# Tiles 8 to 15 of x transposed by VectorE blocks and sixteen SBUF transfers, in a kernel whose task order is written out

## The chip, the cores and the metric

The kernel runs on one core of one Trainium2 chip. The metric is device time in microseconds (us); less is better. Times are medians over runs of one program.

The core has five engines that follow their own instruction queues and wait for each other through semaphores: TensorE (PE in the profile; its weight loads are PEld), VectorE (DVE), ScalarE (ACT), GpSimd (POOL) and SyncE (SP). SBUF is the memory that all work on, in 128 partitions; PSUM holds matmul results in eight banks. Transfers are issued from the queues of SP, ACT and POOL and carried out by 16 DMA engines.

## The reference

```python
S, D, F = 2048, 512, 1792                     # x: [1, S, D] in bf16
g = sigmoid((x * gate_w).sum(-1, keepdims=True))
X = rfft2(x.astype(float32)) * (w_r + 1j * w_i)     # w: [S, D/2+1]
a = irfft2(X, s=(S, D)).astype(bfloat16)
h = x @ w1 + b1                                # w1: [D, F]
b = (h * tanh(softplus(h))) @ w2               # Mish; w2: [F, D]
out = g * a + (1 - g) * b
```

Two branches read the same x: a spectral filter (a two-dimensional real Fourier transform, a product with complex weights W, and the transform back), and a dense layer with Mish between two matrix products. A gate per row mixes them.

## The kernel before, in words

x is held as `xo`, 16 tiles of 128 rows by 512 features. Both branches contract over features first, so they need x with the features in partitions: `xT`, four feature blocks (even and odd features of the lower and the upper half) by 2048 rows. Before, TensorE makes all of `xT`: a matmul with the identity per 128x128 block (L476, tasks `tr0a` to `tr14`, two tiles each), and an eviction from PSUM by DVE (tasks `evx`, L404).

The dense branch goes in four chunks c of 512 rows. `mm1_c_ft` (L773) makes 128 of the 1792 hidden features for a chunk, four matmuls of 128x512 over the four feature blocks; `mish_c_ft` (ACT, L788) evicts them into `act`, which has three buffers, so chunk 3 uses that of chunk 0 again. For chunk 0 the first four are done in parts (`mm1a0_0` and so on, two matmuls of 128x256 each) as x comes in. `mm2_t_part` (L803) makes the output of tile t from 14 hidden blocks, seven with each half of w2; `bev_t` (L755, L756) scales it, `sum_t` adds the spectral part in `ga`, and `store` writes two tiles at a time. Tiles 14 and 15 take `fin` (L815) in one step.

The spectral branch is a chain: `ts`, `td` (DVE, sums and differences of `xT` halves per four tiles), `a1` (L512, transform along features), `eg`, `e1` (evictions), `s1` (L538, first stage along rows), `e2` (eviction), `r1w` (a store to scratch memory), `r1r` (the load back, regrouped, after all sixteen stores), `s2` (L635), `wm` and `wz` (the product with W on DVE and POOL), `s2i` (L695), `e4`, `r2w` and `r2r` (a second trip through scratch), `s1i` (L723), `e5`, `a1i` (L734), `gc`, `sa` (L739, L745) and `sb` (L409, on POOL but for the last tiles), which leave `ga`. The gate comes from `gdot` (DVE, L554), `gpow`, `gadd`, `gcol`, `omg`. `rcw` (L584), `weff`, `wab` prepare edge columns of W.

Nothing decides the order at run time. The program is a list of tasks with their reads and writes (`G.add`); `schedule` reads the string `ORDER`, two digits for each task, with the engine where a task may run on several and the PSUM bank, and appends the task to its engine's queue. Each engine then runs its queue in order, with a wait for each semaphore that a task depends on (L864). A transfer is a task on the queue that issues it (L374); one that waits holds up everything behind it on that queue.

SP's queue begins with x, w1 and the tables, then 18 loads of W (`ld_Wp`, `ld_Wm`, `ld_Wz`), the table `ld_rf`, the two halves of w2 (`ld_w2_0`, `ld_w2_1`), and then the sixteen stores `r1w` and the loads `r1r`.

Of the kernel before, what the change touches and what calls it, by code (L numbers as in the profile page):

```python
# [257 lines left out]
ORDER = (  # L258
    "0M0N0U047050P060O07080Q2z09000S0A010R0B0C0D0T020E0F030V0G0H0W0I0J0X0x60z50Y0yv0Z0K10v1146v212v1H30a1366l51I6q0"
    "14v0L7011Jv6m6n6w1Kv0b716o0c726p731L40d1M36r1N0e1W50f6s6t741Ov1V70g1560h1Pv1X6x0i6y6u16v7510j1Qa1Zv6z0k1701av1"  # L260
    "971Yv77318v761R41Av781B61Sv7920l0m0n7B01fv7A0o7D10p7C1gv0q1D70r1Cv7E1h30s1r42j1s61j7F20t21v0u1Ev7H00v22v1i17G1"
    "T7J31kv7I1U1lv2451F27K7L01mv1t1Gv2371uv7N47M1vv252Ov7O7b127v1wa2D37c2k28a26v7d07f22Nv7e2l1b67g1n42m2E11ca7h22F"
    "7j01d1ov1e7i1x62Hv7k1p342922Gv1ya1q7l52Av2Ia2Q41z2P17m2Z67n0202n2R2b2B2J22Tv7o2a72C2Sv7p12Ka2Uv2cv7r67q2dv2L2V"
    "27s2M2ev7t02Wv2f67u7v12o2X2ga2p7x52Y7w2h2q7z07y2i2r816802s8F1822t3578H48G362u398J28I373A8L58K2v3B8N63C388M0w8P"
    "18O2w8R28Q2x8T02y8S3D4308U3E63Mv8V38X13Nv8W8Y3Rv3Pg313F7P03G323Qv3Og7Q333H3Tg3Z33Sg7Ra3a13b8Z63iv3I57S08a3mv3J"
    "3jv7T3K3L3U3nv3kg3V47Ua7V33c3Xa3Wv3d3pg3Y3e03v43f3og3w644v7W3lg3x3y49v7Y13g7Xv3z3h3q45v7Z48v46g4028307aa4147g3"
    "r4843ta4Bg3sv4Ag3u4H485a4I24Qv86642434J4K4C4Uv4L874Rv89188a4Vv4Sg4D44Wg4M38b24Ea4N4Fa4Tg8c8A4G4Xg8d74O8Ba4P4Y8"
    "C08e4Z28f14av4ba8D8g4c8t18Ev8v28u8x08w4d8z18y4e9124f904g933929549497096992989B79A4h39C4p59D04qv4ia4x64r59E4yv4"
    "j75534s5D45L156a5Ev5T04z65Ma8h24u504t4k5Uv4wg5N14m5F34vg525V55O8i4l9fv5G5Q4ng515b78k04og8jv5W5P54g5I5Sg5H5768l"
    "5ca9ev5853g9g599F75Rg5A8mv5Kg9H49G5Y5Cg5d65X9J09I9hv5e9lv5j45r39K5Jg8n75sv5ka5Bg9kv5g5z35ag9m6745f5l568a5t19iv"  # L270
    "8o60v5m5hg9j5u5o5ig5v6908pa6F45n5Zg6135w8q26Ga5qg629nv6A645pg8r6B9ov635xg9p6C6N46V59qv6Oa9L78sv5yg6Wa66g6P69rv"
    "6X46Q6H26Eg6d09s6Y9M6S6I6Dg6R6ea6K65g6J9O19Nv6Ug6a6Mg6Z9P9uv9tv6cv9v6f56Tg9Qa9R46bv6g9xv6h6Lg9S6i9wv6kv9y9V06j"
    "g9T9U9Y29W9b79X9Z9a9c9d"
)
# [17 lines left out]
def _build(nc, A_x, A_w_r, A_w_i, B_x, B_w1, B_b1, B_w2, gate_w, out):  # L292
# [8 lines left out]
    with es:  # L301
        def sb(name, shape, dt):
            return es.enter_context(nc.sbuf_tensor(name, shape, dt))

        xo = sb("xo", [128, NT, 512], BF)
        xT = sb("xT", [128, 4, NT * 128], BF)
        Tg = sb("Tg", [128, 8192], BF)
# [157 lines left out]

        for t0, h in ((0, 0), (0, 1), (2, 0), (2, 1), (4, None), (6, None), (8, None), (10, None), (12, None), (14, None)):
            pt = _Ps(SPEC[::-1])
            hs = (0, 1) if h is None else (h,)
            c0, nc_ = 2 * hs[0], 2 * len(hs)

            def f_tr(e, t0=t0, c0=c0, nc_=nc_, pt=pt):
                ins = None
                for i in range(2):
                    for c in range(c0, c0 + nc_):
                        o, d0 = ((c - c0) * 2 + i) * 128, 256 * (c // 2) + c % 2
                        ins = e.transpose(psb[:, pt.bank, o:o + 128], xo[:, t0 + i, d0:d0 + 255:2], ident[:, :])  # L476
# [14 lines left out]
        for t in range(NT):  # L491
            if t % 4 == 0:
                G.cur_prio = PR["sp"] + 0.9
                h = t // 4
                cols = slice(512 * h, 512 * h + 512)
                for (nm, o, op) in (("s", 0, ALU.add), ("d", 2, ALU.subtract)):
                    tt(f"t{nm}{h}", lambda o=o, hb=h % 2: Tb[:, hb, o:o + 2, :], lambda cols=cols: xT[:, 0:2, cols],
                       lambda cols=cols: xT[:, 2:4, cols], op, 1024, rate=2.0,
                       reads=[("xT", 4 * h + i, q) for i in range(4) for q in range(2)], writes=[("T", h % 2, nm)])
            if t % 2 == 0:  # L500
# [3 lines left out]
                for half in range(2):  # L504
                    pa = pas[half]

                    def f_a1(e, pa=pa, hb=hb, t=t, half=half):
                        ins = None
                        for i in range(2):
                            j0 = 128 * (t % 4 + i)  # L510
                            for r in range(2):
                                ins = e.matmul(ps[:, pa.bank, 256 * i:256 * i + 256].rearrange("p (s m) -> p s m", s=4)[:, r:4 - r:3 - 2 * r, :],  # L512
                                               Tb[:, hb, 2 * r + half, j0:j0 + 128], FMs[:, 2 * half + r, :], start=True, stop=True)
# [250 lines left out]
        for c in range(NCH):  # L764
            hb = c % 3
            G.cur_prio = PR["mm1"] - c
            for ft in range(NFT):
                pd = _Ps(DENSE[c])

                def f_mm1(e, c=c, ft=ft, pd=pd, cols=(0, 512), ks=range(4)):  # L770
                    ins = None
                    for i in ks:
                        ins = e.matmul(ps[:, pd.bank, cols[0]:cols[1]], w1_sb[:, i, 128 * ft:128 * (ft + 1)], xT[:, i, 512 * c + cols[0]:512 * c + cols[1]],  # L773
                                       start=(i == 0), stop=(i == 3))
                    return ins
# [11 lines left out]
                G.add(f"mish_{c}_{ft}", "act", act_dur(512, True),
                      lambda e, ft=ft, pd=pd, hb=hb: e.activation(act[:, hb, ft, :], ps[:, pd.bank, :], AF.Mish, bias=b1f[:, ft:ft + 1]),  # L788
                      reads=[("pm", c, ft), "b1f"], writes=[("act", hb, ft)], frees=[pd], prio=PR["mish"])
# [148 lines left out]
```

## Time and profile before

| | |
|---|---|
| median of 3 runs | 130.08 us (129.92 to 130.22) |
| profiled execution, first to last instruction | 128.0 us, TensorE's granted clock 1.000 |
| TensorE busy | 124.4 us, 97% |
| DVE, ACT, POOL busy | 92.2, 68.9, 54.4 us |
| moved by DMA | 20.11 MB |

For the profiled execution the profile gives the span alone; what lies around the span is outside the profile. In rows of a group, the columns are the line of the code, engine, operation, output and inputs with their shapes, the count, then busy time in us and the mean of one in ns, then the engine's idle time just before them and what ended it. In the chain and the timelines the columns are start and length in us. "To landing" is the time from the start of a transfer's issue to the arrival of its data. DVE and ACT instructions overlap at their ends: the step from one start to the next is about 0.08 us shorter than the length of one.

### The profile page before, as it was taken

How to read it: one execution, taken by the hardware profiler on the slowest of the kernel's cores; microseconds unless marked ns; L12 is line 12 of the kernel's file. 1: busy time of each engine (PE TensorE's matmuls, PEld its weight loads, DVE VectorE, ACT ScalarE, POOL GpSimd, SP SyncE). 2: the span in 40 equal slices, each digit the busy share in tenths (PEclk: the TensorE clock that was granted, in tenths of full speed). 3: DMA queues.
4: the chain of work that ended last, by engine and by line, in shares of the span. 5: the costliest groups of instructions: out<-in, count | busy, mean ns of one | idle time of the engine just before them, and what ended most of it. 6: DMA issues, size and time to landing. Idle time of an engine off the chain costs nothing.

```text
span 128.0 us, 2725 instructions
## 1 busy us (share of the span) xinstructions
PE 124.4 (97%) x1046; PEld 67.9 (53%) x1046; DVE 92.2 (72%) x176; ACT 68.9 (54%) x113; POOL 54.4 (42%) x82
## 2 busy tenths in 40 slices
PE   7899999999999999999999999999999999999992
PEld 5698566545444444444444444444674457464482
DVE  0359997999989929998957900500399799999872
ACT  1339377889978784224024274487873475462300
POOL 4000000001000996979688394000038986998120
DMA  3999999999976398002304105449600204022231
GB/s 76 346 390 394 303 185 185 173 272 354 334 235 202 99 384 356 0 0 61 108 0 133 38 0 164 133 104 351 239 0 5 82 0 164 3 87 82 82 123 41
DMA packets 18653, 20.11 MB, mean 157 GB/s; under 512 B 1488, under 2 KB 15696, under 8 KB 18512
## 3 DMA queue, kind: packets, MB, share of 16 engines
q1 hardware_dynamic: 17792, 19.15, 49.7%
q10 hardware_dynamic: 816, 0.79, 1.9%
q8 instruction: 8, 0.13, 0.5%
q14 instruction: 5, 0.04, 0.1%
q0 software_dynamic: 32, 0.00, 0.0%
HBM read 13.64 MB, written 6.29 MB: 156 GB/s over the span
## 4 chain that ended last, share of the span: by engine, by line
PE 94%; DMA 3%; SPq 0%; DVE 0%; issue 0%
PE ps L803 38%; PE ps L773 38%; DMA xo<-in_A_x_dram 3%; PE ps L734 3%; PE ps L723 3%; PE ps L512 3%; PE ps L538 3%; PE ps L476 3%; PE ps L695 2%; PE ps L635 2%; SPq L374 0%; DVE xo L815 0%; PE ps L652 0%; PE ps L484 0%; PE ps L425 0%
## 5 line engine op out<-in xcount | busy, mean ns | idle before, releaser
L773 PE MATMUL ps<-xT,w_sb 128*128 128x512 bf16 (+1 forms) x240 | 52.9, 365 | 0.0
L803 PE MATMUL ps<-w_sb,act 128*128 128x512 bf16 (+2 forms) x252 | 51.6, 355 | 0.0
L788 ACT ACTIVATE act<-ps,b1f 128x512 bf16<-128x512 f32 x56 | 38.4, 688 | 18.5 <-PE ps L773 17.3
L803 PEld LDWEIGHTS ps<-w_sb,act 128*128 128x128 bf16 x252 | 22.7, 98 | 22.3 <-issue 0.8
L773 PEld LDWEIGHTS ps<-xT,w_sb 128*128 128x128 bf16 x240 | 22.3, 98 | 21.2 <-issue 0.6
L409 POOL TENSOR_TENSOR Tg<-Qb 128x256 bf16<-128x256 f32 x29 | 22.1, 790 | 21.9 <-DVE Qb L745 21.8
L409 POOL TENSOR_TENSOR Zb<-Qb 128x510 bf16<-128x510 f32 x16 | 19.8, 1268 | 5.1 <-DVE Qb L409 5.0
L409 DVE TENSOR_TENSOR Qb<-ps,WT 128x1024 f32<-128x1024 f32 x16 | 18.8, 1213 | 3.4 <-PE ps L635 3.4
L755 ACT ACTIVATE xo<-ps,omg 128x512 bf16<-128x512 f32 x8 | 5.5, 687 | 18.4 <-PE ps L803 10.1
L745 DVE SCALAR_TENSOR_TENSOR Qb<-ps,gcol,Qb 128x256 f32<-128x256 f32 x32 | 13.7, 475 | 1.5 <-ACT Qb L739 1.0
L404 DVE CAST Ybuf<-ps 128x1024 bf16<-128x1024 f32 x7 | 8.6, 1222 | 7.1 <-PE ps L695 6.7
L409 DVE TENSOR_TENSOR Abuf<-ps,Tg 128x512 bf16<-128x512 f32 x16 | 10.4, 685 | 2.4 <-PE ps L512 2.1
L576 POOL COPY wrv<-WT 128x32 bf16<-128x32 bf16 x2 | 0.4, 223 | 26.1 <-DMA WT<-in_A_w_i_dram 26.1
L405 ACT ACTIVATE Ybuf<-ps 128x1024 bf16<-128x1024 f32 x9 | 9.1, 1021 | 4.3 <-PE ps L695 4.3
L554 DVE SCALAR_TENSOR_TENSOR Tg<-xo,Tg 128x512 bf16<-128x512 bf16 x16 | 11.0, 688 | 0.3
L404 DVE CAST Zb<-ps 128x512 bf16<-128x512 f32 x6 | 4.1, 687 | 8.9 <-PE ps L723 8.9
L404 DVE COPY xT<-ps 128x1024 bf16<-128x1024 bf16 (+1 forms) x10 | 5.6, 579 | 5.4 <-PE ps L476 5.4
L409 DVE TENSOR_TENSOR xo<-xo,Tg 128x512 bf16<-128x512 bf16 x14 | 8.5, 615 | 0.3 <-ACT xo L755 0.3
L739 ACT ACTIVATE Qb<-ps,gcol 128x256 f32<-128x256 f32 x16 | 7.0, 475 | 2.7 <-PE ps L734 1.6
L405 ACT ACTIVATE Zb<-ps 128x512 bf16<-128x512 f32 x10 | 5.7, 596 | 4.6 <-PE ps L723 3.2
L598 POOL TENSOR_TENSOR ch<-wq 128x32 f32<-128x32 f32 x1 | 0.6, 624 | 12.5 <-DVE wq L593 12.5
L476 PE MATMUL ps<-ident,xo 128*128 128x128 bf16 x64 | 5.1, 225 | 0.5 <-DMA xo<-in_A_x_dram 0.5
(59 smaller groups left out, 92.8 us busy)
## 6 DMA issues: line engine op xcount, KB each, us to landing
Abuf<-scr SPq DMA_DIRECT2D x8, 512.0 KB, 5.4
scr<-Ybuf SPq DMA_DIRECT2D x16, 128.0 KB, 3.9
scr<-Ybuf SPq DMA_DIRECT2D x4, 512.0 KB, 3.8
w_sb<-in_B_w_dram SPq DMA_DIRECT2D x2, 896.0 KB, 13.6
out_dram<-xo SPq DMA_DIRECT2D x7, 256.0 KB, 2.0
xo<-in_A_x_dram SPq DMA_DIRECT2D x3, 512.0 KB, 7.7
rt<-c_rt SPq DMA_DIRECT2D x2, 512.0 KB, 8.5
WT<-in_A_w_r_dram SPq DMA_DIRECT2D x7, 128.5 KB, 10.4
```

The source lines that it names most:

```text
L404: fs = {"dve": ("dve", dve_dur(n, rate=rate), lambda e: e.tensor_copy(out=dst(), in_=src())), "act": ("act", act_dur(n), lambda e: e.activ ...
L405: "act": ("act", act_dur(n), lambda e: e.activation(dst(), src(), AF.Copy))}
L409: f = lambda e: e.tensor_tensor(out=o(), in0=i0(), in1=i1(), op=op)
L476: ins = e.transpose(psb[:, pt.bank, o:o + 128], xo[:, t0 + i, d0:d0 + 255:2], ident[:, :])
L512: ins = e.matmul(ps[:, pa.bank, 256 * i:256 * i + 256].rearrange("p (s m) -> p s m", s=4)[:, r:4 - r:3 - 2 * r, :], Tb[:, hb, 2 * r + half ...
L554: lambda e, t=t: e.scalar_tensor_tensor(out=junk, in0=xo[:, t, :], scalar=1.0, in1=gwb, op0=ALU.mult, op1=ALU.mult, accum_out=gdot[:, t:t ...
L739: lambda e, t=t, sl=sl, p5=p5: e.activation(gC[:, sl, :].rearrange("p (i n) -> p i n", i=2), ps[:, p5.bank, :].rearrange("p (i n) -> p i n ...
L745: lambda e, t=t, sl=sl, p5=p5, o=o, op=op: e.scalar_tensor_tensor(out=st1[:, sl, o::2, :], in0=ps[:, p5.bank, :].rearrange("p (i n) -> p i ...
L755: G.add_multi(f"bev_{t}", [("act", act_dur(512, True), lambda e: e.activation(xo[:, t, :], ps[:, pd.bank, :], AF.Copy, scale=omg[:, t:t + ...
L773: ins = e.matmul(ps[:, pd.bank, cols[0]:cols[1]], w1_sb[:, i, 128 * ft:128 * (ft + 1)], xT[:, i, 512 * c + cols[0]:512 * c + cols[1]], sta ...
L788: lambda e, ft=ft, pd=pd, hb=hb: e.activation(act[:, hb, ft, :], ps[:, pd.bank, :], AF.Mish, bias=b1f[:, ft:ft + 1]),
L803: ins = e.matmul(ps[:, pd.bank, cs_], act[:, hb, ft, 128 * tl:128 * (tl + 1)], w2_sb[:, ft, cs_], start=(ft == 0), stop=(ft == NFT - 1))
```

## The change

Tiles 0 to 7 of x are transposed as before, into the first half of `xT`. For tiles 8 to 15, each of eight `tp` tasks is one DVE transpose of a whole tile in blocks of 32x32, written to the third buffer of `act`, where Mish of chunk 2 has not yet written. Block by block this leaves rows and features exchanged inside each 32x32 block, but the blocks in the wrong partitions. Sixteen transfers `sh`, one for each pair of 32-partition groups, 64 KB each, put them in place in the second half of `xT`; each waits for all eight transposes. POOL issues eight and ACT eight. The second half of `xT` has another order of rows (32-row groups of all tiles together), so `ts` and `td` of tiles 8 to 15 become two DVE instructions each, `mm1` of chunks 2 and 3 reads through a pattern, and their Mish puts the rows back in order. Every reader of tiles 8 to 15 waits for all sixteen transfers, and so do the first eight Mish of chunk 2, which overwrite the buffer.

`gdot` gets two scratch outputs in turn, loses its wait for the end of `e1`, and `mm2_15` waits for the other tiles of its chunk.

`ORDER` is new throughout. The engine queues that follow from it differ among other things in this: `mm1a0_1` and `mm1a0_0` stand ahead of the transposes of tiles 2 and 3; all `tp` stand on DVE ahead of the evictions of tiles 4 to 7 (`tp9 tp10 e1p_2 tp11 tp8 tp13 tp12 tp14 tp15 evx6 evx4 e1m_2 td1 ts1 e2_0`); ACT runs `mish_0_8 sh12 sh30 sh32 sh33 mish_0_12 sh13 sh10 mish_1_5 sh31 mish_1_2 sh11 eg_6`; SP runs `ld_gw ld_Wp00 r1w0a`, the other loads of W with `r1w0b` and `ld_ri` among them, then `r1w6b ld_rf r1w6a r1w4a ld_w2_0 ld_w2_1` and the other stores; and TensorE has `mm2_3_0` directly behind `s1_14`, ahead of `s1_10` and `s1_12`.

```diff
 ORDER = (
...
 )
-GD_N = 8
+SHQ = ("pool", "act", "pool", "act")
...
-        xT = sb("xT", [128, 4, NT * 128], BF)
+        xT = sb("xT", [128, 8192], BF)
...
-        junk = Tg[:, 6144:6656]
+        junk = (Tg[:, 6144:6656], Tg[:, 7168:7680])
...
+        xTp = xT[:, 0:4096].rearrange("p (q s) -> p q s", q=4)
+        xTb = xT[:, 4096:8192].rearrange("p (a q t j) -> p q a t j", a=4, q=4, t=8)
+        Zb32 = act[:, 2].rearrange("p f s -> p (f s)")[:, 0:4096]
+        Zw = Zb32.rearrange("p (b h e t j) -> p t h b e j", b=4, h=2, e=2, t=8)
...
-        for t0, h in ((0, 0), (0, 1), (2, 0), (2, 1), (4, None), (6, None), (8, None), (10, None), (12, None), (14, None)):
+        for t0, h in ((0, 0), (0, 1), (2, 0), (2, 1), (4, None), (6, None)):
...
+        for t in range(8, NT):
+            G.add(f"tp{t}", "dve", dve_dur(512), lambda e, t=t: e.transpose(
+                Zw[:, t - 8], xo[:, t, :].rearrange("p (b j e) -> p b e j", b=8, e=2)),
+                reads=[("x", t)], writes=[("Z", t)])
+        shs = []
+        for b in range(4):
+            for a in range(4):
+                shs.append(dma(f"sh{b}{a}", xT[32 * b:32 * b + 32, 4096 + 1024 * a:5120 + 1024 * a], Zb32[32 * a:32 * a + 32, 1024 * b:1024 * b + 1024],
+                               reads=[("Z", t) for t in range(8, NT)], writes=[("xB", b, a)], nbytes=65536, queue=SHQ[b], tail=1.9, bw=250e3))
+        XB = [("xB", b, a) for b in range(4) for a in range(4)]
...
+                    for e_ in range(2):
+                        xs = [xTb[:, e_ + 2 * i, :, 4 * h - 8:4 * h - 4, :] for i in range(2)]
+                        tt(f"t{nm}{h}{e_}", lambda o=o, e_=e_, hb=h % 2: Tb[:, hb, o + e_, :].rearrange("p (t a j) -> p a t j", t=4, a=4),
+                           lambda xs=xs: xs[0], lambda xs=xs: xs[1], op, 512, rate=2.0,
+                           reads=XB, writes=[("T", h % 2, nm, e_)])
...
-            G.cur_prio = PR["gate"] if t >= GD_N else 60.0
+            G.cur_prio = PR["gate"]
...
-                  reads=[("x", t), "gw"], writes=[("gd", t), "junk"], lock=True, deps=e1s[14] if t >= GD_N else ())
+                  reads=[("x", t), "gw"], writes=[("gd", t), ("junk", t % 2)], lock=True)
...
+                        o = ps[:, pd.bank, cols[0]:cols[1]]
+                        ins = e.matmul(o if c < 2 else o.rearrange("p (a t j) -> p a t j", a=4, t=4), w1_sb[:, i, 128 * ft:128 * (ft + 1)],
+                                       xTp[:, i, 512 * c + cols[0]:512 * c + cols[1]] if c < 2 else xTb[:, i, :, 4 * c - 8:4 * c - 4, :],
                                        start=(i == 0), stop=(i == 3))
...
+                      lambda e, c=c, ft=ft, pd=pd, hb=hb: e.activation(
+                          act[:, hb, ft, :].rearrange("p (t a j) -> p t a j", t=4, a=4),
+                          ps[:, pd.bank, :].rearrange("p (t a j) -> p t a j" if c < 2 else "p (a t j) -> p t a j", t=4, a=4),
+                          AF.Mish, bias=b1f[:, ft:ft + 1]),
+                      reads=[("pm", c, ft), "b1f"], writes=[("act", hb, ft)], frees=[pd], prio=PR["mish"],
+                      deps=shs if c == 2 and ft < 8 else ())
...
-                       alloc=pd if part == 0 or t == NT - 1 else None, deps=(mm2s[c][-1:] if t == NT - 1 and part else []))
+                       alloc=pd if part == 0 or t == NT - 1 else None, deps=(mm2s[c][-1:] if t == NT - 1 else []))
```

More of the change, by code (lines that the diff above doesn't have):

```diff
@@ L258 @@
 ORDER = (
[L259 to L273, printed above, removed]
+    "0M0P040050600070Q0108090A0B0C0D0N0E0F0G0H0I0x10J0yv0R0O0K0U020S0z50L7A37511120T031347F612v10a7K70V7614v0W7B1av"
@@ new lines @@
+    "1X01Zv7L0X1Y77787G797H7C1c21l47M1b51n7R01d1ev7D1fv7E7P11gv7V41A7Q7I1m20Y7N7T51B1ov1C1737S7b17h07O7X7197W1E7U1D"
+    "1F0Z1G7J7f418v0a7c1557Z616v7i7Y1N1R1h00b1T1pv1Q1V1W1wv8178538D51vv1iv1S7g1O2842721J7z0341qv1L861U807v1833361j1"
+    "M290c7x038330d7w8B22Bv3A1K7d10e0f820g1H0h7y1I7a1x72Ca1P0i1z1k2Av8H0352Iv8C2Jv1y40w8768j77e8Z220v8p10j8I2Hv883J"
+    "21v2L02Kv8422v2gv2V68E3C0k2D32W50l2fv0m8k2N2M72X8d02hv0n0o2Yv0p2Ea2Zv0q8F62Pv8J38q0r2342iv8a2Ov8G8e24v0s2t12u2"
+    "1r62Qv2G0t2v1sa3O8L02F372xv252ya8t52R62j18f42wv2l0u8M2Sv3E8g8r22k00v2z62av2nv398u7s12b430a2mv1t2oa3B3P68s8n72T"
@@ new lines @@
+    "1u2U8K2p232263G313Q2ca2qv3D7p08h67q2e8943F8v52d3H8o8b72r3I2s8A8c8i7m23T3R3K7t8w3X33S3V3Y63L3M8l58m7n3a7j53Z3hv"
+    "3gv3b3c33U3N3jg7ua3lv7ra3kv7k3ig7la3u03t63d7oa3mg9F43w3ng3v8Q33x8z543v8R9042v46v9G8Sa3y744g3e45g47v4F44G09J24P"
+    "v8x68W33z4H4I4Ov3f3W8y49g3o3p4408X4148g4Sv9K4J4A4Qg3qa3rv4Tv4B49N29L04Ca3s4K14Dv4b44L4Rg4kv4c64Ug4M9O9D28T18Ya"
+    "4Vg4e4d4f4g34N4W9M4lv8U4ng4h4E9V04i9E4pv4mg4ov4rg4X24Za9464j954Ya4qg4s8Vv4a9W4t14vv9108N79T54ua9d1929P29Z39Q4w"
+    "9e9U9H48O9I4x51252a4y5919X55345P29a93v5Av5B08Pv5X15H3977544z565Qa5596a5n25C5Iv5J45Ya5R65f39Y5K5v15E5Z55D5S5ov5"
@@ L496, in _build @@
                 for (nm, o, op) in (("s", 0, ALU.add), ("d", 2, ALU.subtract)):
-                    tt(f"t{nm}{h}", lambda o=o, hb=h % 2: Tb[:, hb, o:o + 2, :], lambda cols=cols: xT[:, 0:2, cols],
-                       lambda cols=cols: xT[:, 2:4, cols], op, 1024, rate=2.0,
-                       reads=[("xT", 4 * h + i, q) for i in range(4) for q in range(2)], writes=[("T", h % 2, nm)])
+                    if h < 2:
+                        tt(f"t{nm}{h}", lambda o=o, h=h: Tb[:, h, o:o + 2, :], lambda cols=cols: xTp[:, 0:2, cols], lambda cols=cols: xTp[:, 2:4, cols], op, 1024, rate=2.0,
+                           reads=[("xT", 4 * h + i, q) for i in range(4) for q in range(2)], writes=[("T", h, nm, e) for e in range(2)])
+                        continue
+                    for e_ in range(2):
[3 more added lines that the diff above has]
+                           reads=XB, writes=[("T", h % 2, nm, e_)])
             if t % 2 == 0:
@@ L514, in f_a1 @@
                         return ins
-                    pe(f"a1{half}_{t}", 4 * mm(128), f_a1, reads=[("T", hb, "s"), ("T", hb, "d"), "FD"], writes=[("pa", t, half)], alloc=pa,
+                    pe(f"a1{half}_{t}", 4 * mm(128), f_a1, reads=[("T", hb, nm, half) for nm in "sd"] + ["FD"], writes=[("pa", t, half)], alloc=pa,
                        deps=e1s.get(t - 4, ()) if half == 0 else (), prio=PR["sp"] + 0.1 - 0.1 * half)
@@ L784, in _build @@
                 else:
-                    pe(f"mm1_{c}_{ft}", 4 * mm(512), f_mm1, reads=[("xT", 4 * c + i, q) for i in range(4) for q in range(2)] + [("w1", ft, 0), ("w1", ft, 1)],
+                    pe(f"mm1_{c}_{ft}", 4 * mm(512), f_mm1, reads=(XB if c >= 2 else [("xT", 4 * c + i, q) for i in range(4) for q in range(2)]) + [("w1", ft, 0), ("w1", ft, 1)],
                        writes=[("pm", c, ft)], alloc=pd, deps=mm2s.get(c - 3, ()), prio=pr_m)
                 G.add(f"mish_{c}_{ft}", "act", act_dur(512, True),
-                      lambda e, ft=ft, pd=pd, hb=hb: e.activation(act[:, hb, ft, :], ps[:, pd.bank, :], AF.Mish, bias=b1f[:, ft:ft + 1]),
-                      reads=[("pm", c, ft), "b1f"], writes=[("act", hb, ft)], frees=[pd], prio=PR["mish"])
+                      lambda e, c=c, ft=ft, pd=pd, hb=hb: e.activation(
[4 more added lines that the diff above has]
+                      deps=shs if c == 2 and ft < 8 else ())
             G.cur_prio = PR["mm2"] - c
```

9 lines of the change are left out of this document (6 added, 3 removed).

## The prediction

> **What bounds the kernel now.** I read the page first (busy shares, chain), then the chain of waits in order of time, then the engines' timelines around each moved step.
>
> ```profile
> span 128.0 us, 2725 instructions
> ...
> PE 124.4 (97%) x1046; PEld 67.9 (53%) x1046; DVE 92.2 (72%) x176; ACT 68.9 (54%) x113; POOL 54.4 (42%) x82
> ...
> PE 94%; DMA 3%; SPq 0%; DVE 0%; issue 0%
> ```
> ```profile
> 5.57 0.40 PE ps L476 x4
> ...
> 7.12 1.75 PE ps L773 x16
> ...
> 12.16 0.89 PE ps L476 x16
> ...
> 20.23 0.22 PE ps L512 x4
> 20.45 0.86 PE ps L773 x4
> ...
> 26.75 0.87 PE ps L538 x4
> ...
> 47.36 0.56 PE ps L635 x32
> ...
> 49.75 3.02 PE ps L803 x14
> ...
> 79.14 0.57 PE ps L695 x32
> ...
> 90.83 0.45 PE ps L723 x8
> ...
> 119.56 6.13 PE ps L803 x56
> ...
> 125.71 0.35 DVE xo L815
> ```
>
> The chain is one engine. From 5.57, when tiles 2 and 3 of x have landed, to 125.69 (119.56 + 6.13) TensorE never waits for anybody; DVE, ACT and POOL feed it just in time. So matmul time that goes away is time gained, but nothing stands idle that could swallow a new wait: a transfer or an eviction that comes later than TensorE reaches its reader is lost time in full.
>
> **What is removed.** The program of after has 32 of the 64 transposes (L476). The chain prices sixteen at 0.89, so 32 cost 1.78 us. Two two-matmul groups of L773 also move ahead of the transposes of tiles 2 and 3, into the wait for x: four matmuls of 128x256 at 1.75/16 are 0.44, of which I count 0.3, since they overrun the landing a little. TensorE: -2.1 us. Four DVE evictions of 1024 columns go too.
>
> **What is added on VectorE.** Eight 32x32-block transposes, 512 columns each, `tp13 tp12 tp14 tp15` being the last four; they stand in front of the evictions `evx6` and `evx4` of tiles 6, 7, 4, 5.
>
> ```profile
> L374 SPq DMA_DIRECT2D xo<-in_A_x_dram x1: 777/777/777, 5.5 to 5.5; - x1
> ...
> DMA to landing us min/median/max: 9.5/9.5/9.5
> ```
> ```profile
> 4.85 0.76 DVE L404 COPY xT<-ps 128x512 bf16<-128x512 bf16 x2 [4.85 <-PE ps L476]
> ...
> 9.83 1.29 DVE L409 TENSOR_TENSOR Abuf<-ps,Tg 128x512 bf16<-128x512 f32 x2 [1.41 <-PE ps L512]
> ...
> 13.02 1.28 DVE L404 COPY xT<-ps 128x1024 bf16<-128x1024 bf16 x2
> 14.39 1.22 DVE L404 CAST Ybuf<-ps 128x1024 bf16<-128x1024 f32 x1
> ```
>
> No row shows this transpose. Below, it costs what a packed 512-column copy does (two in 0.76: 0.34 from start to start); above, what a 1024-column cast does (1.2). I take the 512-column row that moves one element at a time: two in 1.29, so 0.6 from start to start, 0.69 in all. Tiles 12 to 15 land at 5.5 + 9.5 = 15.0 (the loads ahead of them are the same), so the four end at 15.0 + 4 x 0.6 + 0.1 = 17.5, and the two evictions (0.6 each) at 18.8. When does TensorE want them? At `mm1_1_3`. I count its queue from 5.7: 24 transposes (1.33), 28 matmuls of 256 (3.06), nine `mm1` of four (20.45 row: 0.864 each, 7.78), four `a1` groups (0.22 each), `s1_0` (26.75 row: half of 0.87) and one small one: 13.5, so 19.2. (The same count over before's queue meets 49.75 within 0.3.) Hidden, with 0.4 to spare; at 1.2 each the four end at 19.9, the evictions at 21.2, and 2.0 us are lost. [...]
>
> **The sixteen transfers.** Each waits for all eight transposes. Eight are issued by POOL, eight by ACT between its Mish evictions.
>
> ```profile
> L374 POOL DMA_DIRECT2D braw<-in_B_b_dram x1 | 0.8, 785 | 0.8 <-POOLq L923 0.8
> ```
> ```profile
> 0.80 1.94 ACTq L374 DMA_DIRECT2D w_sb<-in_B_w_dram  x3
> ...
> 11.61 1.28 ACT L788 ACTIVATE act<-ps,b1f 128x512 bf16<-128x512 f32 x2
> ```
> ```profile
> out_dram<-xo SPq DMA_DIRECT2D x7, 256.0 KB, 2.0
> ...
> w_sb<-in_B_w_dram ACTq DMA_DIRECT2D x3, 256.0 KB, 4.9
> ```
> ```profile
> L864 PEldq EVENT_SEMAPHORE  x30: 51/51/517, 2.8 to 103.6; - x30
> ```
>
> First reader on TensorE is `mm1_2_5`: eleven `mm1` (9.5) and four `a1` groups (0.9) behind `mm1_1_3`, so 29.6. POOL: 0.785 an issue in the one row there is (a smaller load); I take 0.9, so the eighth issue starts at 17.5 + 6.3 = 23.8. Landing of 64 KB inside SBUF has no row; between the 2.0 of a quiet store and the 4.9 of a load in a full queue I take 3 from the issue's start: 26.8. ACT: eight issues at 0.65 (5.2), seven Mish at 0.6 and 1.2 of smaller evictions reach `eg_4`, whose bank `mm1_2_5` takes, at 28.1. Both hidden; POOL's margin, 2.8, is gone when an issue costs over 1.3, and each 0.1 beyond is 0.7 lost. Sixteen semaphores are read two at a time: eight wait instructions of 0.051 with gaps, 0 to 0.8, taken as 0.3, as only a matmul or two cover them.
>
> **What moves on SP's queue** is the dear part. Before, all eighteen loads of W, then both halves of w2, stand ahead of the first store to scratch. In after, `r1w0a` stands behind the first load of W, and `r1w0a` waits for `e2_0`, which DVE reaches behind the transposes: 17.5, two evictions, three more 0.6 steps and a cast of 1.2: 21.8. Seventeen loads of W queue behind it. And `ld_w2_0` stands behind `r1w4a`, which waits for `e2_4`, the eviction of `s1_4`.
>
> ```profile
> 7.55 5.84 SPq L374 DMA_DIRECT2D WT<-in_A_w_r_dram  x9
> 13.43 6.73 SPq L374 DMA_DIRECT2D WT<-in_A_w_i_dram  x9
> ...
> 20.82 2.59 SPq L374 DMA_DIRECT2D w_sb<-in_B_w_dram  x2
> ```
> ```profile
> 14.50:27.00 12.50, 12.50 (x96) 7.11 (x94) 11.76 (x22) 8.89 (x17) 0.00 (x0) 1.00 1.11 185
> ```
> ```profile
> L374 SPq DMA_DIRECT2D scr<-Ybuf x8: 614/616/617, 35.4 to 40.0; - x8
> ```
> ```profile
> L374 SPq DMA_DIRECT2D Abuf<-scr x1: 344/344/344, 42.3 to 42.3; - x1
> ...
> DMA to landing us min/median/max: 4.0/4.0/4.0
> ```
> ```profile
> L374 SPq DMA_DIRECT2D Abuf<-scr x1: 432/432/432, 43.6 to 43.6; - x1
> ...
> DMA to landing us min/median/max: 6.7/6.7/6.7
> ```
>
> Seventeen issues at 0.65 to 0.75 end SP's work on W at 34 to 36, which its reader (`rcw`, near 44) can bear. For w2: TensorE starts `s1_4` 6.5 us behind `mm1_2_5` (six `mm1`, four `a1`, `s1_6`), at 36.4 with the 0.3; it is done at 37.0, `e2_4` (1.22) at 38.2, `r1w4a` is issued by 38.9. A 512 KB load alone landed after 4.0, and of the four such loads the last landed 4.0 later than the first, 1.33 each; 896 KB then take 5.0: 43.9. Its reader `mm2_3_0` stands 6.1 behind the start of `s1_4`: 42.5. That is a wait of 1.4 with an empty queue. The queue isn't empty: in the row of 14.5 to 27 us, W kept the sixteen engines full at 185 GB/s, so the 2 MB of W from 23 on, with half of the new transfers, one table and two stores among them (3.3 MB in all), end near 41 at that rate; a table of 512 KB and three stores stand directly ahead of w2. I take a wait of 1.9. Ends: 0 (w2 lands in 3.3) and 4. Before, the w2 loads were issued at 20.8 and first read at 49.75: that cover is what is spent.
>
> **What gets tighter behind it.** From the first `s2` to the last `s2i` TensorE has 28.4 us of work in after, 31.8 before (47.36 to 79.14); from the first `s1i` to its end 27.9 against 34.9 (90.83 to 125.69).
>
> ```profile
> L409 POOL TENSOR_TENSOR Zb<-Qb 128x510 bf16<-128x510 f32 x16 | 19.8, 1268 | 5.1 <-DVE Qb L409 5.0
> ...
> L756 DVE TENSOR_SCALAR xo<-ps,omg 128x512 bf16<-128x512 f32 x6 | 4.5, 746 | 1.2 <-PE ps L803 1.2
> ```
> ```profile
> 90.80:126.00 35.20, 34.87 (x285) 21.07 (x282) 30.70 (x63) 16.27 (x33) 22.08 (x29) 1.00 0.18 68
> ```
>
> DVE was busy 30.7 us of the last stretch. After, three of its L756 evictions (0.75) and two steps of the 0.6 kind lie elsewhere: 27.3 of about 28, with the last products still to wait for. POOL's 19.8 us of `wz` lie in 28.4 instead of 31.8. I take 0.4 for both, between 0 and 1.5.
>
> **The sum**, against the profiled execution's span: -2.1 + 0.3 + 1.9 + 0.4 = +0.5, so 128.5. The span stands 2.1 under the median of the runs, 130.08, and I leave that as it is: 130.6 us.
>
> **Rivals.** First, w2 lands in time, because 896 KB come faster than the scratch reads did, or `e2_4` ends sooner: then -2.1 + 0.3 + 0.4, 128.7 us, and 128.0 if the small terms vanish. For it: W's pace may be only that of its issues. Against: the count of 6.1 us from `s1_4` to `mm2_3_0` holds no place for eviction, store issue and a 5 us load. Second, slower than before: POOL's issues. From 1.3 us each they decide; at 1.6 the last transfer starts at 28.7, lands at 31.7 and `mm1_2_5` stalls 2.1; the w2 wait follows along at 1.4, as `s1_4` is as late as its reader: -2.1 + 2.1 + 0.3 + 1.4 + 0.4, 132.2. For it: the one price there is comes from a smaller load, and the profile calls POOL's spans rough. Against: it would have to be 1.7 times that row. [...] Third, the block transpose at 1.2: 130.6 + 2.0, 132.6.
>
> **How the numbers follow.** Forecast (w2 wait near 1.9, the rest hidden) 0.45; w2 in time 0.30; POOL late 0.17; dear transpose 0.08. Three runs spread by 0.2%, so less than that, 0.26 us, can't be told from no change. The first rival and the cheap edge of the forecast are faster: 0.34; same 0.11; slower 0.55. Range 128.2 (first rival, nearly all small terms at nothing) to 133.2; the forecast's own is 129.6 to 131.6.
>
> **What would show it.** Right: TensorE's wait list has L803 waiting about 2 us for a DMA of w2 near 43 us, and L773 waits for the new transfers well under 1 us near 30. The transposes on DVE show 0.69. Wrong: L803 never waits for a load (first rival); POOL's DMA rows over 1.2 (second); DVE rows of 1.1 or more (third); or a longer DVE-ruled tail than 0.5.

## The result, and the profile after

| | before | after |
|---|---|---|
| median, 4 runs each | 130.00 us | 135.78 us (135.15 to 136.47) |
| ratio after to before, 95% interval | | 1.0448 (1.0399 to 1.0497) |
| profiled execution: time, span, granted clock | 128.0 span, 1.000 | 135.15, 133.4 span, 0.982 |

The change made the kernel 4.5% slower. The prediction, 130.6 us with a range to 133.2, was too low. First the page of the kernel after, with the row of the granted clock over 40 slices of the span:

```profile
span 133.4 us, 2728 instructions
...
PE 124.5 (93%) x1014; PEld 66.6 (50%) x1014; DVE 91.8 (69%) x179; ACT 69.1 (52%) x117; POOL 57.2 (43%) x91
...
PEclk9999999999999959999999999999999999999997
...
PE 80%; DMA 9%; DVE 7%; issue 1%; DVEq 0%; SPq 0%
```

TensorE was 97% busy, and the chain was 94% its own; now a DMA holds 9% of the chain and VectorE 7%. TensorE has 32 matmuls fewer and the same busy time: some of them ran at a lower clock. The slice with the 5 tells where. The waits of TensorE (total, times, longest, us) and the chain in order of time (start, length):

```profile
PE ps L830 <- DMA w_sb<-in_B_w_dram: 4.0, 1, 4.0
```
```profile
37.68 0.88 DVE Ybuf L409
...
39.74 7.47 DMA w_sb<-in_B_w_dram
...
47.26 3.05 PE ps L830 x7
...
52.09 1.51 PE ps L830 x7
...
122.17 1.65 DVE Qb L766 x4
...
130.72 0.26 DVE xo L842
```

Three places differ from before. At 43 us TensorE waits 4.0 us for w2 (L830 is `mm2`, L803 before). Behind that wait the seven matmuls of `mm2_3_0` take 3.05 us; the next seven of this kind take 1.51, and in the kernel before they took 1.51 to 1.62. And from 122 us on the chain runs through VectorE to the end, where before it was TensorE's up to the last 0.35. The windows around the wait (busy us of PE, PEld, DVE, ACT, POOL with instruction counts, then the granted clock, the DMA share and GB/s), and SP's queue:

```profile
42.00:44.00 2.00, 1.29 (x9) 0.51 (x7) 1.74 (x5) 1.95 (x4) 0.00 (x0) 1.00 0.98 304
44.00:46.00 2.00, 0.00 (x0) 0.00 (x0) 2.00 (x7) 1.59 (x4) 0.00 (x0) 1.00 0.97 315
46.00:48.00 2.00, 0.74 (x2) 0.28 (x3) 0.01 (x1) 0.00 (x0) 0.00 (x0) 0.66 1.02 326
48.00:50.00 2.00, 2.00 (x6) 0.76 (x5) 0.00 (x0) 0.00 (x0) 0.00 (x0) 0.50 1.12 341
```
```profile
22.70 0.65 SPq L379 DMA_DIRECT2D scr<-Ybuf  x1
...
30.00 7.04 SPq L379 DMA_DIRECT2D WT<-in_A_w_i_dram  x9
...
37.76 0.60 SPq L379 DMA_DIRECT2D rt<-c_rt  x1
38.41 1.29 SPq L379 DMA_DIRECT2D scr<-Ybuf  x2
39.74 1.60 SPq L379 DMA_DIRECT2D w_sb<-in_B_w_dram  x2
```

`r1w0a` is issued at 22.70, the last load of W is through at 37.04 (30.00 + 7.04), and w2 follows a table and the stores up to `r1w4a`. The DMA engines are full from 42 us on, and the granted clock is 0.66 and then 0.50 of full speed in the two windows in which the matmuls resume.

The new work itself, the block transposes on VectorE and the issues and landing of the transfers, costs about what was thought, or less:

```profile
14.32 3.66 DVE L489 STREAM_TRANSPOSE act<-xo 128x512 bf16<-128x512 bf16 x6
```
```profile
L379 ACTq DMA_DIRECT2D xT<-act x8: 514/604/613, 18.0 to 24.3; - x8
L379 POOL DMA_DIRECT2D xT<-act x8: 496/497/552, 18.3 to 21.7; - x8
...
who waited for it (us, times):
  ACT act L811: 2.7, 4
...
DMA to landing us min/median/max: 2.0/2.6/3.8
```

No matmul waits for a transfer; ScalarE does, four times, which delays nothing on the chain.

### The profile page after: what moved, and what is told of

Read it like the earlier page. It is cut to its first block, busy times and chain, and to the rows that moved or that the text cites. A ratio compares the mean times of both kernels' runs of the same rounds, so it can differ in the third digit from the quotient of the medians.

```text
span 133.4 us, 2728 instructions
## 1 busy us (share of the span) xinstructions
PE 124.5 (93%) x1014; PEld 66.6 (50%) x1014; DVE 91.8 (69%) x179; ACT 69.1 (52%) x117; POOL 57.2 (43%) x91
## 3 DMA queue, kind: packets, MB, share of 16 engines
q1 hardware_dynamic: 17792, 19.15, 46.7%
## 4 chain that ended last, share of the span: by engine, by line
PE 80%; DMA 9%; DVE 7%; issue 1%; DVEq 0%; SPq 0%
PE ps L795 34%; PE ps L830 32%; DMA w_sb<-in_B_w_dram 9%; PE ps L755 3%; PE ps L744 3%; DVE xo L414 2%; PE ps L533 2%; PE ps L716 2%; PE ps L656 2%; PE ps L559 2%; DVE Qb L766 2%; DVE Tg L414 1%; DVE xo L842 1%; PE ps L481 1%; DVE Ybuf L409 1%
## 5 line engine op out<-in xcount | busy, mean ns | idle before, releaser
L830 PE MATMUL ps<-w_sb,act 128*128 128x512 bf16 (+2 forms) x252 | 53.2, 362 | 4.0 <-DMA w_sb<-in_B_w_dram 4.0
L811 ACT ACTIVATE act<-ps,b1f 128x512 bf16<-128x512 f32 x56 | 35.6, 692 | 28.1 <-PE ps L795 22.9
L830 PEld LDWEIGHTS ps<-w_sb,act 128*128 128x128 bf16 x252 | 23.1, 99 | 28.3 <-DMA w_sb<-in_B_w_dram 4.5
L414 POOL TENSOR_TENSOR Tg<-Qb 128x256 bf16<-128x256 f32 x30 | 23.4, 815 | 16.3 <-DVE Qb L766 16.2
L766 DVE SCALAR_TENSOR_TENSOR Qb<-ps,gcol,Qb 128x256 f32<-128x256 f32 x32 | 13.5, 473 | 0.3 <-ACT Qb L760 0.3
L776 ACT ACTIVATE xo<-ps,omg 128x512 bf16<-128x512 f32 x11 | 7.4, 687 | 7.6 <-PE ps L830 6.4
L379 POOL DMA_DIRECT2D xT<-act x8 | 4.0, 504 | 15.9 <-DVE act L489 15.9
L414 DVE TENSOR_TENSOR xo<-xo,Tg 128x512 bf16<-128x512 bf16 x14 | 9.2, 678 | 0.0
L410 ACT ACTIVATE Zb<-ps 128x512 bf16<-128x512 f32 x11 | 6.6, 602 | 1.3 <-PE ps L744 1.3
L409 DVE COPY xT<-ps 128x512 bf16<-128x512 bf16 (+1 forms) x5 | 2.5, 521 | 6.9 <-PE ps L481 6.9
L414 DVE TENSOR_TENSOR Tg<-xT 128x512 bf16<-128x512 bf16 (+1 forms) x12 | 5.7, 506 | 0.5 <-issue 0.5
L409 DVE CAST Zb<-ps 128x512 bf16<-128x512 f32 x5 | 3.4, 683 | 3.8 <-PE ps L744 3.8
## 6 DMA issues: line engine op xcount, KB each, us to landing
scr<-Ybuf SPq DMA_DIRECT2D x16, 128.0 KB, 4.1
```

Source lines behind the costliest of these rows:

```text
L409: fs = {"dve": ("dve", dve_dur(n, rate=rate), lambda e: e.tensor_copy(out=dst(), in_=src())), "act": ("act", act_dur(n), lambda e: e.activ ...
L410: "act": ("act", act_dur(n), lambda e: e.activation(dst(), src(), AF.Copy))}
L414: f = lambda e: e.tensor_tensor(out=o(), in0=i0(), in1=i1(), op=op)
L766: lambda e, t=t, sl=sl, p5=p5, o=o, op=op: e.scalar_tensor_tensor(out=st1[:, sl, o::2, :], in0=ps[:, p5.bank, :].rearrange("p (i n) -> p i ...
L776: G.add_multi(f"bev_{t}", [("act", act_dur(512, True), lambda e: e.activation(xo[:, t, :], ps[:, pd.bank, :], AF.Copy, scale=omg[:, t:t + ...
L811: lambda e, c=c, ft=ft, pd=pd, hb=hb: e.activation(act[:, hb, ft, :].rearrange("p (t a j) -> p t a j", t=4, a=4), ps[:, pd.bank, :].rearra ...
```

## The experiments

The order is a string, so an edit of it is shown as the queue that it makes, `...` for what is left out. Times are medians, and each ratio is to the kernel before on the same chip.

**1. w2 early.** Theory: the late w2 and the cold clock are the whole loss.

```diff
 SP: ld_gw ld_Wp00
+    ld_w2_0 ld_w2_1
     r1w0a ld_Wm00 ... ld_Wz1 r1w6b ld_rf r1w6a r1w4a
-    ld_w2_0 ld_w2_1
     r1w2a ...
```

> The changed kernel with one edit: both loads of w2 stand on SP's queue directly behind the first load of W, ahead of the first store to scratch, instead of behind the last one. Theory L (the late w2 costs its wait and the cold clock behind it): TensorE's 4.0 us idle at mm2_3_0 and the 1.5 us that its seven matmuls took longer at the granted clock of 0.5 to 0.66 both vanish, the rest keeps its place: 135.8 - 5.5 = 130.3 us, and TensorE waits under 0.5 us for w2. Theory C (the 16 transfers, W and the scratch traffic load the DMA engines so much that something else is late, or DVE and POOL in the last stretch set the end whenever TensorE arrives): less than 3 us come back, over 132.8, and the idle time stands in front of another row.

Measured: 129.61 us (10 runs), ratio to before 0.9985 (0.9965 to 1.0005). Theory L holds: 6.2 us come back, more than the 5.5 expected, and C falls. TensorE's waits, the start of `mm2_3_0` in the chain and the transfers' landing in this kernel:

```profile
PE ps L430 <- PEq L950: 0.8, 1, 0.8
PE ps L830 <- DVE xo L777: 0.2, 1, 0.2
```
```profile
43.23 1.29 PE ps L830 x6
```
```profile
DMA to landing us min/median/max: 5.3/5.7/6.1
```

The sixteen transfers now share the DMA engines with w2 and land after 5.7 instead of 2.6 us, and nobody on the chain notices. But with the wait gone the kernel only equals the one before: 1.78 us of transposes left TensorE, and 0.2 of it shows, which the interval can't tell from nothing. Where the rest went is the question of experiments 4, 8, 9 and 10.

**2. Only the second half early.** Is the first half late because it shares with the second?

```diff
 SP: ... ld_Wp00
+    ld_w2_1
     r1w0a ... r1w4a ld_w2_0
-    ld_w2_1
     r1w2a ...
```

> The changed kernel with one edit: only the second half of w2 is loaded early, the first half stays where it is, behind the last store to scratch. Theory S (the first half's landing of 7.5 us comes from sharing the engines with the second half, issued 0.7 us behind it): alone it lands in about 5, the wait at mm2_3_0 is about 1.9 instead of 4.0, the clock falls less, about 132 to 133 us. Theory B (it waits for what was queued before it, a table and three stores): it still lands about 7 us after its issue, the wait stays near 3.5 to 4, 134.5 to 135.8.

Measured: 135.73 us, ratio 1.0442 (1.0411 to 1.0474). Theory S falls. The wait and the chain of this kernel:

```profile
PE ps L830 <- DMA w_sb<-in_B_w_dram: 4.6, 1, 4.6
```
```profile
39.10 8.28 DMA w_sb<-in_B_w_dram
```

Without the second half right behind it, the first took 8.28 us instead of 7.47, so the second half isn't what makes it late. (The stores to scratch behind it then move up, so this run doesn't show that nothing behind counts.)

**3. TensorE kept busy while it waits.** Two things cost time at that place, the wait and the clock. This one leaves w2 where it is and fills the wait.

```diff
+        pk = [t for t in G.tasks if t.name in ("s1_14", "eg_12")]
+        def f_keep(e):
+            ins = None
+            for _ in range(19):
+                ins = e.matmul(ps[:, 1, :], nc.const_aps.tensor(1.0, [128, 128], BF), xTp[:, 0, 0:512], start=True, stop=True)
+            return ins
+        pe("keep", 0.1, f_keep, deps=pk)
...
 PE: ... s1_14
+    keep
     mm2_3_0 ...
```

> The changed kernel with one addition: 19 matmuls of 128x512 that nobody reads (their bank is overwritten by mm2_3_0) run on TensorE while it waits for w2. Theory K (the granted clock falls because TensorE stood idle for 4 us): the clock stays at 1.0 from 43 to 50 us, mm2_3_0's seven matmuls take about 1.5 instead of 3.05, and the time is 1.5 us lower, 134.2. Theory T (the clock falls for another reason, a throttle that heavy DMA or long load brings): mm2_3_0 still takes about 3, and the time stays at 135.8 or is higher.

Measured: 133.58 us, ratio 1.0293 (1.0239 to 1.0347): 2.2 less than the changed kernel. In the chain (L860 is the added line) and the page:

```profile
44.06 2.75 PE ps L860 x12
46.81 1.67 PE ps L830 x7
```
```profile
PEclk9999999999999999999999999999999999999999
```

Theory K holds: w2 takes as long (7.8 us from its issue to its landing), the clock stays at 1.00, and `mm2_3_0` takes 1.67 instead of 3.05. Between the two profiled executions that is 1.3 us (135.15 and 133.81), between the medians 2.2. Two of the four runs of the changed kernel took 135.2 at a mean clock of 0.982 to 0.985 and two 136.4 at 0.974; how long the clock was low in the latter two, no trace here shows. With the wait of 4.0 the 2.2 are the 6.2 of experiment 1.

The traces show when the clock falls, read in windows of 0.2 us. In the changed kernel the last matmul before the wait ends at 43.3, the clock falls from 1.00 to 0.50 at 46.6, and it is back at 50.0. In experiment 2 these three times are 42.8, 46.7 and 50.1, in the second kernel of experiments 6 and 7 below (a wait of 4.2) 30.4, 35.5 and 38.9. Each time the low clock lasts 3.4 us. It starts 3.4, 3.8 and 5.2 us after the last matmul, the last time one microsecond after the matmuls have resumed. So how much of it falls on work differs from one execution to the next.

**4. The front.** `mm1a0_1` and `mm1a0_0` moved ahead of `tr2a`; does it cost or gain?

```diff
 (experiment 1, and)
 PE: ...
-    mm1a0_1 mm1a0_0 tr2a tr2b
+    tr2a tr2b mm1a0_1 mm1a0_0
     ...
```

> The kernel with both loads of w2 early, and beside it the transposes of tiles 2 and 3 (tr2a, tr2b) stand ahead of the two matmul groups mm1a0_1 and mm1a0_0, as before the change. Theory F (the front lost time because the two groups wait for the first load of w1 to land near 6 us): the first stretch of the chain becomes as before the change, tr2a at 5.6 instead of 6.6, worth 0.4 to 0.6 us: 129.7 to 129.9, if w2 early gives 130.3. Theory E (the last stretch is set by DVE and POOL, which swallow it): within 0.2 of the other kernel.

Measured: 129.61 us, ratio 0.9986 (0.9966 to 1.0006), the same as experiment 1. The chain of experiment 1, then that of this one:

```profile
5.52 0.95 PE ps L795 x4
6.47 0.53 PE ps L481 x8
...
9.40 0.45 PE ps L533 x8
```
```profile
5.53 0.86 PE ps L481 x8
...
9.34 0.45 PE ps L533 x8
```

Whichever comes first is drawn out by what it waits for (0.95 for two groups that take 0.44, 0.86 for transposes that take 0.45), and by the first `a1` (L533) 0.06 us are left. The front neither gained nor lost; theory F falls.

**5. The table behind w2.** What stands ahead of w2 in the queue?

```diff
 SP: ... r1w6b
-    ld_rf
     r1w6a r1w4a ld_w2_0 ld_w2_1
+    ld_rf
     r1w2a ...
```

> The changed kernel with one edit: the load of a table of 512 KB (ld_rf) that SP issues 2.0 us ahead of w2 is moved behind both loads of w2, which keep their place behind r1w4a. Theory Q (w2_0 lands late because all that is in flight shares some 300 GB/s with it, the table's 512 KB among it): SP reaches w2_0 0.6 earlier only if it isn't held by r1w4a, and 512 KB at 300 GB/s are 1.7 us less ahead of it; the wait at mm2_3_0 falls from 4.0 to 2.0 to 2.8, and with a shorter cold clock the time falls by 1.5 to 2.5 us, to 133.3 to 134.3. Theory N (the table doesn't matter, w2_0's own 896 KB need their 7.5 us): the wait stays at 3.7 to 4.3, the time at 135.5 to 135.9.

Measured: 131.70 us, ratio 1.0148 (1.0118 to 1.0177). Theory Q holds in kind, and the effect is larger than it said: 4.1 us come back instead of at most 2.5, and the wait of 1.9 is just under its 2.0 to 2.8. The wait and the chain:

```profile
PE ps L830 <- DMA w_sb<-in_B_w_dram: 1.9, 1, 1.9
```
```profile
39.34 5.60 DMA w_sb<-in_B_w_dram
...
44.99 1.47 PE ps L830 x6
```

One table of 512 KB, 2.0 us ahead in the queue, was worth 2.1 us of wait, and since the clock stayed at 1.00 with this wait of 1.9 us (`mm2_3_0` in 1.47), it was worth the 2.2 us of clock too; the sum of both is 4.3. What was ahead counted: the first half of w2 took 8.28 us with the table ahead of it and without the second half right behind it (experiment 2), and 5.60 with the table and the second half both behind it.

**6 and 7. W without a stop.** Two stores stand among W's loads and hold it; both kernels move them behind W, the second with w2 early.

```diff
 SP: ... ld_Wp00
-    r1w0a
     ld_Wm00 ...
-    r1w0b
     ld_ri ... ld_Wz1
+    r1w0a r1w0b
     r1w6b ...
```

> The changed kernel with one edit: the first two stores to scratch (r1w0a, r1w0b), which stand among the loads of W on SP's queue, are moved behind the last of W's eighteen loads, so that W is issued without a stop from 17 to about 30 us; w2 stays behind r1w4a. Theory W (it is W's loads, issued as late as 37 us because r1w0a holds them, that fill the engines when w2 is issued): W is gone by 36, w2_0 lands 5 to 5.5 after its issue, the wait is 1.5 to 2.2 instead of 4.0, the clock falls less, time 132.3 to 133.3. Theory N (W has landed by then anyway, and only what is issued within 2 us of w2 shares with it): the wait stays at 3.5 to 4.3 and the time at 135 to 135.9.

Measured with w2 late: 133.12 to 137.77 us in four runs, too wide for a ratio, so the time gives no verdict between W and N. Its profiled execution (133.12) shows a new wait beside that for w2:

```profile
PE ps L830 <- DMA w_sb<-in_B_w_dram: 1.9, 1, 1.9
PE ps L795 <- DMA xT<-act: 1.5, 1, 1.5
```
```profile
40.94 5.61 DMA w_sb<-in_B_w_dram
```

In this execution w2 lands in 5.61 us with the table still ahead of it. But the new wait puts `s1_4` back to 38.60 (37.21 in the changed kernel) and the issue of w2 with it, while the table is issued at 37.59. So the table is 3.35 us ahead instead of 2.0, and it lands 0.8 us after w2's issue instead of 2.6. This suggests that what counts is how much of the table is still under way when w2 is issued. The wait of 1.9 is theory W's number, but its cause isn't shown by it: in the changed kernel the last load of W has landed at 39.5, before w2 is issued. No trace shows the other three executions.

The second kernel takes the w2 wait out and so prices the new one alone.

> SP's queue nearly in the order of before the change: both loads of w2 and all eighteen loads of W ahead of the first store to scratch; all else as changed. Theory X (W in flight from 17 to 36 us shares the DMA engines with the sixteen transfers inside SBUF, which then land after 5 to 7.5 us instead of 2 to 3.8): TensorE waits 1 to 2.5 us for them at mm1_2_5 near 30 us, 130.6 to 132.2 against 129.61. Theory Y (the transfers come in time with W in flight too): under 0.3 of wait, 129.3 to 129.9.

Measured: 131.46 us, ratio 1.0115 (1.0094 to 1.0136); 1.9 us above experiment 1. Theory X holds in kind. The profiled execution took 135.30 us at a clock of 0.987, with a wait of 4.2 us and 3.4 us of the clock at 0.50 behind it, so its rows show the kind of the wait, not the size that goes with 131.46:

```profile
PE ps L795 <- DMA xT<-act: 4.2, 1, 4.2
```
```profile
DMA to landing us min/median/max: 8.2/9.2/10.4
```

With W in flight the transfers land after 9.2 us at the median instead of 2.6 (after 8.8 in the execution of 133.12 above, where the wait was 1.5), later than the 5 to 7.5 of theory X, and `mm1_2_5` waits. So there is a price on each side: `r1w0a` in front of W keeps the engines free for the sixteen transfers, and the same hold pushes W and then w2 back.

**8. Two evictions to ScalarE.** In experiment 1, the stretch from the first `s1i` to the last product (96.24 to 125.41 us) has VectorE busy for 28.34 of 29.17 us:

```profile
96.24:125.41 29.17, 27.78 (x250) 17.92 (x249) 28.34 (x58) 17.39 (x36) 23.37 (x30) 1.00 0.21 79
```

```diff
 (experiment 1, and)
-DVE: ... e5_10 ... e5_11 ...
+ACT: ... e5_9 e5_10 gc_9 e5_13 e5_11 gc_7 ...
```

> The kernel with both loads of w2 early (129.61 us), and beside it two evictions of the last stretch, e5_10 and e5_11 (0.6 a step on VectorE), go to ScalarE. Theory D (from 100 us on VectorE is the bound: 20.0 busy of 20 us, its last products end 1.2 us behind TensorE's last matmul): 1.2 us less on VectorE, the last product then follows TensorE's last matmul by about 0.4, time 0.7 to 0.9 lower, 128.7 to 128.9. Theory P (GpSimd, busy 21.6 of 21.9 us from 99.4 to 121.2, or ScalarE's column products are as tight): less than 0.3 lower, 129.3 to 129.6.

Measured: 130.07 us, ratio 1.0021 (1.0000 to 1.0042): 0.5 slower than experiment 1, outside both theories. VectorE lost the 1.2 us of work and stood idle for most of it, waiting for ScalarE, whose column products `gc` now queue behind the two evictions:

```profile
105.56 1.66 DVE L766 SCALAR_TENSOR_TENSOR Qb<-ps,gcol,Qb 128x256 f32<-128x256 f32 x4 [0.57 <-ACT Qb L760]
...
109.22 0.87 DVE L766 SCALAR_TENSOR_TENSOR Qb<-ps,gcol,Qb 128x256 f32<-128x256 f32 x2 [0.28 <-ACT Qb L760]
```

**9. The order of the last products.** Less work on VectorE at its end, none added to ScalarE. Before the edit GpSimd idles there, and VectorE runs two sums of tile 14 ahead of what GpSimd waits for (experiment 1, the timelines of GpSimd and of VectorE):

```profile
122.38 1.83 POOL L414 TENSOR_TENSOR Tg<-Qb 128x256 bf16<-128x256 f32 x2 [1.15 <-DVE Qb L766]
```
```profile
119.70 1.81 DVE L414 TENSOR_TENSOR Tg<-Qb 128x256 bf16<-128x256 f32 x2
```

The end of TensorE's work in experiment 1, and the last two products in its chain:

```profile
114.88 9.30 PE L830 MATMUL ps<-w_sb,act 128*128 128x512 bf16 x70
```
```profile
124.89 0.52 DVE xo L842 x2
```

```diff
 (experiment 1, and)
 DVE: ... sum_10 sum_9
-     sbm_14 sbp_14 sam_15 sap_15
+     sam_15 sap_15 sbm_14
      sum_11 fin_14_1 ...
 POOL: ... sbm_13
+     sbp_14
      sbp_15 sbm_15
```

> The kernel with both loads of w2 early, and beside it, in the last stretch: the products sa of tile 15 stand on VectorE ahead of the sums sb of tile 14 (0.9 each), and one of these two goes to GpSimd, which waits there 1.15 us for tile 15's products. Theory D (VectorE's own order sets the end: it is busy without a break from 100 to 125.4 us and ends 1.2 us behind TensorE's last matmul): 0.9 less on it, the last product 0.5 to 0.9 us earlier, 128.7 to 129.1 against 129.61. Theory P (GpSimd, busy from 99.4 us with 30 sums of 0.75, sets it): no earlier than its own end, 99.4 + 31 x 0.75 + 0.3 = 123 plus the products behind it, 129.4 to 129.8.

Measured: 128.82 us (6 runs), ratio 0.9929 (0.9909 to 0.9949). It is 0.7% below the kernel before, and 5% below the changed one. GpSimd now runs through, and the last product follows TensorE's last matmul by 0.82 us (123.71 + 0.99 against 114.58 + 9.30) instead of 1.23 (124.89 + 0.52 against 114.88 + 9.30):

```profile
114.58 9.30 PE L830 MATMUL ps<-w_sb,act 128*128 128x512 bf16 x70
```
```profile
109.73 13.44 POOL L414 TENSOR_TENSOR Tg<-Qb 128x256 bf16<-128x256 f32 x17 [0.28 <-DVE Qb L766]
```
```profile
123.71 0.99 DVE L842 SCALAR_TENSOR_TENSOR xo<-ps,omg,Tg 128x256 bf16<-128x256 f32 x3
```

Theory D holds: the last product ends 0.7 us earlier (124.70 for 125.41). TensorE too ended 0.3 earlier here, which the edit doesn't explain and which lies within what executions of this kernel differ by; the other 0.4 is the new order's.

**10. Both.** The order of 9 with the two evictions of 8, and `sum_1` moved up into VectorE's idle time.

```diff
 (experiment 9, and)
-DVE: ... sam_6 e5_10 sam_5 ... sum_4 e5_11 sum_3 ... sap_7 sum_1 sam_9 ...
+DVE: ... sam_6 sum_1 sam_5 ... sum_4 sum_3 ... sap_7 sam_9 ...
+ACT: ... e5_9 e5_10 gc_9 e5_13 e5_11 gc_7 ...
```

> The kernel of the last stretch reordered, and beside it the two evictions e5_10 and e5_11 on ScalarE, with one sum (sum_1) moved up to where VectorE then stood idle for 0.57 us. Theory D: another 0.3 to 0.6 us off VectorE's last 15 us, 128.4 to 128.8. Theory P or a bound by TensorE's own end (124.2 us, last product 0.35 and last store about 2 behind): the same as the kernel beside it within 0.2.

Measured: 129.39 us, ratio 0.9983 (0.9962 to 1.0004), 0.6 slower than 9, again outside both theories. As in 8, VectorE waits for the column products that queue behind the evictions on ScalarE:

```profile
109.27 1.27 DVE L766 SCALAR_TENSOR_TENSOR Qb<-ps,gcol,Qb 128x256 f32<-128x256 f32 x3 [0.77 <-ACT Qb L760]
```

## Why the prediction was wrong

**The bound.** TensorE as the one chain was right, and so was the warning that a transfer later than its reader is lost in full.

**Removed, -2.1.** Of the 1.78 for the transposes, 1.5 can be seen where nothing else interferes: in experiment 1 TensorE's last matmul ends at 124.18, before at 125.69. The 0.3 for the two groups moved ahead isn't there (experiment 4): w1 and x land so close together that either order waits.

**Block transposes.** 0.6 from start to start was taken and 0.61 measured (3.66 us for six). The last ended at 18.0; 17.5 was forecast.

**The transfers.** An issue on POOL was taken at 0.9 and took 0.50; landing at 3, and it was 2.0 to 3.8. `mm1_2_5`, the second of the four groups that the chain has in one piece from 29.84 to 33.29, started at 30.70 with no wait. It was forecast for 29.6, and `mm1_1_3` came at 20.31 instead of 19.2: the counted work took 13.7 us for 13.5, but it began at 6.61, behind the two groups moved ahead, and not at 5.7. The 0.3 for reading sixteen semaphores isn't there: no gap in this kernel, 0.2 in that of experiment 4. The rivals "POOL late" and "dear transpose" fall by these rows.

**w2, the step that failed.** The mechanism, the place and the reader's time (42.5 forecast; 43.2 when it doesn't wait, in experiment 1) were right. The size was not. The prediction put it as: "896 KB then take 5.0: 43.9", "a table of 512 KB and three stores stand directly ahead of w2. I take a wait of 1.9". So the table was seen and then charged, with all the rest of the queue, 0.5 us. It costs 2.1 where it stands: behind w2 instead, it leaves a landing of 5.60 and a wait of 1.9 (experiment 5), by chance the very figure that was forecast with it ahead; ahead of w2, it is 7.47 and 4.0. In the changed kernel it landed at 42.4, 2.6 us after w2 was issued, and the first half of w2 4.9 later. W's loads were issued until 37.04, not 34 to 36. The issue of w2 was 0.8 late (39.74 for 38.9), as `s1_4` was (37.21 for 36.4), but the reader was 0.7 late too, so that adds only 0.1 to the wait.

**The clock, a term that was missing.** The profile of before can't show it, since TensorE has no such wait there. A wait of 4.0 us cost 2.2 more at the medians (experiment 3), of which 1.5 stand in the profiled execution as 3.05 instead of 1.51; a wait of 1.9 cost none. The granted clock was 0.50 behind the wait of 4.0 and 1.00 behind the one of 1.9. The range's end of 4 for the wait was thus no end of its price: the wait of 4.0 had a second one, which the forecast has no term for.

**The last stretch, 0.4.** It was between 0 and 1.5, and is 1.3 in experiment 1: the last product ends 1.23 us behind TensorE instead of 0.37 (126.06 - 125.69), and from there to the end of the span it is 2.4 us instead of 1.9, as the last three products come in one bunch and SP ends the issue of their stores 0.9 us behind them instead of 0.4. (The span of experiment 1 is 127.8, that of before 128.0.) That VectorE would be tight there was in the text, and its count was right: 27.3 us of work in 28, and 27.12 in the 27.94 from the first `s1i` to TensorE's end in experiment 1. Only the price was taken too low. (The 28.4 us counted from the first `s2` to the last `s2i` measured 29.2; no wait of note follows from that.) That one sum on GpSimd and another order of the last four tasks take half a microsecond and more out of it, only experiment 9 showed.

**The sum.** Forecast: -2.1 + 0.3 + 1.9 + 0.4 = +0.5. Measured: experiment 1 is 0.2 below before, the wait is 4.0 and the clock 2.2: +6.0, and the medians differ by 5.8. What was missed: 2.1 by the wait's size, 2.2 by the clock, and 1.2 by the other terms, where -1.4 was forecast and -0.2 came: 0.9 for the last stretch, 0.3 for the front and 0.3 for the part of the transposes that doesn't show, less 0.3 for the semaphores. The first rival, w2 in time, is experiment 1: 128.7 was worked out for it and 129.61 measured.

## What to carry to other kernels

A load that is moved behind a store which itself waits for computed data has to be priced with all the bytes ahead of it in its queue, one by one; here a single table in front made the wait twice as long (4.0 us for 1.9). A wait of the matmul engine can have two prices, the wait and a lower clock behind it: here the wait of 4.0 us had the clock at 0.50 behind it and cost 2.2 us more, and the wait of 1.9 left the clock at 1.00; so look first for what shortens such a wait, even if it can't be removed. And where the bounding engine gets shorter, the gain is only there if the engines that finish behind it are put in order too: the same change with w2 early was worth nothing, and with a few tasks of the last stretch rearranged it was worth 0.7%.

## What was not expected of the hardware

- The granted clock fell to 0.50 in the waits of 4.0, 4.6 and 4.2 us or just behind them, for 3.4 us each time, and stayed at 1.00 with waits of 1.9; with matmuls in the gap that nobody reads (experiment 3) it stayed at 1.00 too.
- A 64 KB transfer inside SBUF landed after 2.0 to 3.8 us in the changed kernel, where the DMA engines were busy for a share of 0.02 in the 2 us ahead of the first, after 5.3 to 6.1 with w2 in flight (experiment 1), and after 8.2 to 10.4 with W in flight (in the execution of 135.30 us).
- An issue by GpSimd took 0.50 us, less than one by ScalarE in the same stretch (0.51 to 0.61) and than the single one of before (0.785).
